# Gate and val products of the second MLP by Strassen's seven block products over pairs of token blocks

## The chip, the cores and the metric

The kernel runs on one core of one Trainium2 chip. The metric is the device time of one execution in microseconds (us). The kernel before was timed three times: 1830.27, 1833.56 and 1836.62 us, median 1833.56 us. A separate execution was profiled.

## The reference

Attention over pooled keys feeds two MLPs, and only the last result is returned:

```python
x = attention(q, pool8(k), pool8(v))          # 4608 tokens x 512
h = x @ w_in                                  # 512 x 2048
x = where(h >= 1, h, where(h <= -1, 0, (h + 1)**2 / 4)) @ w_out
gate = 1 / (1 + exp(-(x @ w_gate)))           # 512 x 1536
val = x @ w_val                               # 512 x 1536
out = (gate * val) @ w_out2                   # 1536 x 512
```

Every product is made to nearly full float32 accuracy: each operand is split into a high and a low part, and three matmuls (high x high, high x low, low x high) stand for one.

## The kernel before

The 4608 tokens are NB = 9 blocks of 512 columns, the model width 512 is KD = 4 chunks of 128 rows, the second MLP's width is M2 = 12 chunks. `three` (line 564) issues the three matmuls of one 128 x 128 weight block with one 128 x 512 operand; `columns` (line 569) does so for the four chunks of the width and leaves 12 matmuls in one PSUM bank. There are eight banks: four `acc`, two `h`, two `a`.

The first MLP leaves its transposed result of block j in DRAM as `y_d[j]`. The weights of the second MLP are decoded while the first MLP runs and go to DRAM as 36 `spilled` tensors of 256 KB. `reload` (line 503) brings one back, ScalarE (ACT) copies out the high part, VectorE (DVE) subtracts to get the low part. All 36 are reloaded once: eight into pool `w2a`, which opens when attention's pools are closed (`open_a`), sixteen into the slots of the first MLP's `win`, twelve into `w2b`, which opens when the first MLP's pools `wout` and `wj` are closed (`open_b`). From then on the weights stay in SBUF.

The loop from line 692 on goes over nine blocks and twelve m. For one m it issues 12 matmuls for gate into an `h` bank, 12 for val into an `a` bank, then sigmoid on ACT (line 700), the product with val on DVE (line 702), high part on ACT (line 491) and low part on DVE (line 500) into `g`, and two steps later 12 matmuls of `g` with `w2[2, m]` into the four `acc` banks. `x2_load` (line 674) fetches the next block's `y_d` in two DMAs. `out_rows` copies `acc` out and stores it.

The order of the instructions is not that of the code. Every operation goes to a `Plan` with an engine, a cost and a due time (`key`); `Plan.issue` lists them: on each engine, of those that could start first, the one with the smallest key goes next. The engines then run that order as it stands. SP issues the loads and stores, POOL the loads and spills of the second MLP's weights; each waits in order too.

Of the kernel before, what the change touches and what calls it, by code (L numbers as in the profile page):

```python
# [64 lines left out]
class Plan:  # L65
# [130 lines left out]
def pooled_attention_two_mlps(  # L196
# [53 lines left out]
    def buf_x(dtype=F32R, shape=(P, 2, TB)):  # L250
        return Buf(x_p, "x", 2 * KD, list(shape), dtype)
# [252 lines left out]
    def reload(d, t, key, behind):  # L504

        vals = Src(t, lambda t: t[:, 1].bitcast(F32))
        op(SP, 0.475, key - AHEAD_RELOAD, lambda: nc.sync.dma_start(out=vals(), in_=d.t),
           r=[d], w=[t], behind=behind, nbytes=P * DM * 4)
        op(ACT, 0.62, key - 2, lambda: nc.scalar.copy(out=t.t[:, 0], in_=vals()), r=[t], w=[t])
        op(DVE, 0.69, key - 1, lambda: nc.vector.tensor_tensor(  # L510
            out=t.t[:, 1], in0=vals(), in1=t.t[:, 0].bitcast(F32), op=ALU.subtract), r=[t], w=[t])
# [49 lines left out]
        return t.t.rearrange("p s (c f) -> p s c f", c=KD)  # L561


    def three(o, wh, wl, xh, xl, start, stop):
        nc.tensor.matmul(out=o, lhsT=wh, rhs=xh, start=start, stop=False)  # L565
        nc.tensor.matmul(out=o, lhsT=wh, rhs=xl, start=False, stop=False)  # L566
        nc.tensor.matmul(out=o, lhsT=wl, rhs=xh, start=False, stop=stop)  # L567

    def columns(key, o, w, xs):
        last = []  # L570
# [103 lines left out]
    def x2_load(j, key):
        raw = [buf_x(F32) for _ in range(2)]
        for i, r in enumerate(raw):
            op(SP, 0.475, key, lambda i=i, r=r: nc.sync.dma_start(
                out=r.t, in_=y_d[j].t[2 * i * P:2 * (i + 1) * P, :].rearrange("(c p) t -> p c t", p=P)),
                r=[y_d[j]], w=[r], nbytes=P * DM * 8)
        return raw  # L680

    def x2_split(raw, key):
        xs = []
        for c in range(KD):
            x, src = buf_x(), Src(raw[c // 2], lambda t, c=c: t[:, c % 2])
            high_part(key, x, src)
            low_part(key, x, src)
            xs.append(x)
        return xs

    xs = x2_split(x2_load(0, due1((NB - 1) * M1)), due1(NB * M1 - 2))
    for j in range(NB):
        raw = x2_load(j + 1, due2(j, 0)) if j + 1 < NB else None
        for m in range(M2):
            T = due2(j, m)
            pg, pv = bank("h", True), bank("a", True)
            columns(T, pg, w2[0, m], xs)
            columns(T + 2.6, pv, w2[1, m], xs)
            t, g = Buf(t_p, "t", 2, [P, TB]), buf_g()
            op(ACT, 0.48, T + 5, lambda t=t, pg=pg: nc.scalar.activation(out=t.t, in_=pg.t, func=AF.Sigmoid),  # L700
               r=[pg], w=[t])
            op(DVE, 0.6, T + 6, lambda t=t, pv=pv: nc.vector.tensor_tensor(  # L702
                out=t.t, in0=pv.t, in1=t.t, op=ALU.mult), r=[t, pv], w=[t])
            high_part(T + 7, g, Src(t))
            low_part(T + 8, g, Src(t))
            if m == 0:
                accs = [bank("acc") for _ in range(4)]
                last_o = [[] for _ in range(4)]
            w = w2[2, m]
            for c in range(4):  # L710
                def mm(c=c, w=w, g=g, m=m, accs=accs):
                    three(accs[c].t, g.t[:, 0, c * P:(c + 1) * P], g.t[:, 1, c * P:(c + 1) * P],
                          w.t[:, 0], w.t[:, 1], m == 0, m == M2 - 1)
                last_o[c] = [op(PE, 0.65, T + 2 * S2 + 5.2 + 0.1 * c, mm, r=[w, g], w=[accs[c]], behind=last_o[c])]
        if raw:
            xs = x2_split(raw, due2(j + 1, 0) - 1)
        out_rows(T + 2 * S2 + 6, out[j * TB:(j + 1) * TB, :], accs)
# [33 lines left out]
```

## Time and profile before

| what | value |
|---|---|
| times of three executions | 1830.27, 1833.56, 1836.62 us |
| profiled execution | 1831.4 us, of which 1829.6 us lie between first and last instruction (the span) |
| TensorE (PE) busy | 1787.8 us, 8096 matmuls of all sizes |
| weight loads (PEld) busy | 1447.3 us |
| DVE, ACT, POOL busy | 856.5, 763.1, 46.2 us |
| DMA | 122.01 MB, mean 67 GB/s |
| mean granted clock of TensorE | 0.993 of full speed |

Busy time is the sum over an engine's instructions where they don't overlap. Matmuls are pipelined: each lasts longer than the distance to the next. The granted clock is 1.00 at 2.4 GHz and 0.50 at 1.2 GHz; a mean between them is a mixture of the two.

### The profile page before, as it was taken

Reading aid. Unit: us, or ns where it says so; the run is one execution under the profiler, and the core shown is the slowest. Engines: PE = TensorE matmul, PEld = TensorE weight load, DVE = VectorE, ACT = ScalarE, POOL = GpSimd, SP = SyncE. Lnnn points to the kernel's source line nnn. Section 1 sums busy time; section 2 is a strip of 40 time slices with the busy share of each in tenths; the row PEclk is TensorE's granted clock in tenths of the full one; section 3 lists DMA queues with packets and bytes.
Section 4 is the critical chain, followed back from the end, with each engine's and each line's share of the span. In section 5 each row is a group of like instructions: output and inputs, shape, how many; then the busy total and the mean of one; then the engine's idle time right before and its main releaser. Section 6 shows DMA issues by size and latency. Waiting matters only on the chain.

```text
span 1829.6 us, 21475 instructions
## 1 busy us (share of the span) xinstructions
PE 1787.8 (98%) x8096; PEld 1447.3 (79%) x8096; DVE 856.5 (47%) x1581; ACT 763.1 (42%) x1719; POOL 46.2 (3%) x78
## 2 busy tenths in 40 slices
PE   6789999999999999999999999999999999999998
PEld 4567778888888777878888888888888888888887
DVE  8899767676776866566451212121121212121211
ACT  6766656565666656566561211121121212121111
POOL 0000001010100100010000000000000000000000
PEclk9999999999999999999999999999999999999999
DMA  8632525242433432123140000000010101010000
GB/s 215 203 102 75 144 56 163 60 143 73 133 89 113 115 90 70 59 77 116 47 144 1 23 24 23 24 23 24 1 46 1 46 1 47 0 47 0 1 23 24
DMA packets 136712, 122.01 MB, mean 67 GB/s; under 512 B 82592, under 2 KB 100000, under 8 KB 136608
## 3 DMA queue, kind: packets, MB, share of 16 engines
q1 hardware_dynamic: 128544, 92.32, 17.8%
q0 software_dynamic: 8064, 28.32, 4.6%
q8 instruction: 64, 1.05, 0.2%
q14 instruction: 40, 0.33, 0.1%
HBM read 82.84 MB, written 28.31 MB: 61 GB/s over the span
## 4 chain that ended last, share of the span: by engine, by line
PE 92%; DVE 2%; DMA 2%; ACT 2%; issue 1%; SPq 0%; POOL 0%; DVEq 0%; POOLq 0%; ACTq 0%
PE h L565 12%; PE acc L565 12%; PE acc L567 12%; PE acc L566 12%; PE h L567 12%; PE h L566 12%; PE a L565 5%; PE a L567 5%; PE a L566 5%; PE a L402 2%; PE a L470 2%; DMA win<-in_moe_w_in_dram 1%; DMA raw<-in_moe_w_out_dram 1%; ACT f L537 0%; DMA x<-in_k_dram 0%
## 5 line engine op out<-in xcount | busy, mean ns | idle before, releaser
L702 DVE TENSOR_TENSOR t<-a,t 128x512 f32<-128x512 f32 x108 | 74.7, 692 | 566.0 <-PE a L567 566.0
L567 PE MATMUL h<-x,win 128*128 128x512 f32 x756 | 297.2, 393 | 8.8 <-DVE win L500 8.8
L565 PE MATMUL h<-x,win 128*128 128x512 f32 x756 | 300.5, 398 | 0.0
L566 PE MATMUL h<-x,win 128*128 128x512 f32 x756 | 296.7, 393 | 0.0
L491 ACT CAST g<-t 128x512 fp32r<-128x512 f32 x252 | 156.6, 621 | 331.9 <-DVE t L702 274.1
L565 PE MATMUL acc<-g,wj 128*128 128x512 f32 x576 | 229.5, 399 | 2.1 <-ACT g L491 2.1
L567 PE MATMUL acc<-g,wj 128*128 128x512 f32 x576 | 225.9, 392 | 4.0 <-DVE wj L500 4.0
L700 ACT ACTIVATE t<-h 128x512 f32<-128x512 f32 x108 | 64.8, 600 | 386.7 <-PE h L567 386.7
L566 PE MATMUL acc<-g,wj 128*128 128x512 f32 x576 | 225.3, 391 | 0.2 <-DVE g L500 0.2
L500 DVE TENSOR_TENSOR g<-t,g 128x512 fp32r<-128x512 f32 x252 | 173.6, 689 | 107.5 <-ACT g L491 106.8
L630 ACT ACTIVATE t<-h,half 128x512 f32<-128x512 f32 x144 | 99.3, 689 | 185.7 <-PE h L567 185.7
L567 PEld LDWEIGHTS h<-x,win 128*128 128x128 f32 x756 | 143.2, 189 | 41.6 <-DVE win L500 11.6
L565 PEld LDWEIGHTS h<-x,win 128*128 128x128 f32 x756 | 144.0, 190 | 38.7 <-issue 5.9
L566 PEld LDWEIGHTS h<-x,win 128*128 128x128 f32 x756 | 143.4, 190 | 28.8
L634 DVE SCALAR_TENSOR_TENSOR t<-t,h 128x512 f32<-128x512 f32 x144 | 97.7, 679 | 89.6 <-ACT t L632 89.0
L567 PEld LDWEIGHTS acc<-g,wj 128*128 128x128 f32 x576 | 108.7, 189 | 28.9 <-DVE wj L500 6.1
L565 PEld LDWEIGHTS acc<-g,wj 128*128 128x128 f32 x576 | 109.0, 189 | 25.6 <-ACT g L491 2.5
L566 PEld LDWEIGHTS acc<-g,wj 128*128 128x128 f32 x576 | 108.8, 189 | 22.0 <-DVE g L500 0.5
L500 DVE TENSOR_TENSOR wj<-wout_f,wj 128x512 fp32r<-128x512 f32 x144 | 98.8, 687 | 24.5 <-ACT wj L491 24.5
L491 ACT CAST wj<-wout_f 128x512 fp32r<-128x512 f32 x144 | 89.7, 623 | 32.7 <-PE acc L567 31.8
L632 ACT ACTIVATE t<-t 128x512 f32<-128x512 f32 x144 | 91.2, 633 | 3.4
L565 PE MATMUL acc<-win,g 128*128 128x512 f32 x216 | 84.0, 389 | 0.0
(134 smaller groups left out, 2921.8 us busy)
## 6 DMA issues: line engine op xcount, KB each, us to landing
y<-raw SPq DMA_DIRECT2D x18, 512.0 KB
w<-f POOLq DMA_DIRECT2D x36, 256.0 KB, 2.3
x<-y SPq DMA_DIRECT2D x18, 512.0 KB
out_dram<-raw SPq DMA_DIRECT2D x18, 512.0 KB
win<-in_moe_w_in_dram SPq DMA_DIRECT2D x16, 512.0 KB
raw<-in_moe_w_out_dram SPq DMA_DIRECT2D x16, 512.0 KB
aT<-aq SPq DMA_DIRECT2D x256, 32.0 KB
kv<-in_k_dram SPq DMA_DIRECT2D x28, 288.0 KB
```

Of the source, the lines that this page charges most:

```text
L402: nc.tensor.matmul(out=view()[lo - r0:hi - r0, t].rearrange("p h c -> p (h c)"), lhsT=qT.t[:, lo:hi], rhs=bds[b % 2, p].t, start=True, sto ...
L470: nc.tensor.matmul(out=px.t[D * h:D * h + D, lo:hi], lhsT=vps[b % 2, p].t[:, h], rhs=rhs, start=True, stop=True)
L491: ACT: (0.52, lambda: nc.scalar.copy(out=dst.t[:, 0], in_=src())),
L500: op(engs, [0.6 if e == DVE else 1.23 for e in engs], key, [lambda e=e: by[e].tensor_tensor(out=dst.t[:, 1], in0=src(), in1=dst.t[:, 0].bi ...
L565: nc.tensor.matmul(out=o, lhsT=wh, rhs=xh, start=start, stop=False)
L566: nc.tensor.matmul(out=o, lhsT=wh, rhs=xl, start=False, stop=False)
L567: nc.tensor.matmul(out=o, lhsT=wl, rhs=xh, start=False, stop=stop)
L630: op(ACT, 0.69, Tg, lambda t=t, hps=hps: nc.scalar.activation(out=t.t, in_=hps.t, func=AF.Relu, bias=half.t, scale=0.5), r=[hps, half], w=[t])
L632: op(ACT, 0.63, Tg + 1, lambda t=t: nc.scalar.activation(out=t.t, in_=t.t, func=AF.Square), r=[t], w=[t])
L634: op(DVE, 0.69, Tg + 2, lambda t=t, hps=hps: nc.vector.scalar_tensor_tensor(out=t.t, in0=t.t, scalar=1.0, in1=hps.t, op0=ALU.min, op1=ALU. ...
L700: op(ACT, 0.48, T + 5, lambda t=t, pg=pg: nc.scalar.activation(out=t.t, in_=pg.t, func=AF.Sigmoid), r=[pg], w=[t])
L702: op(DVE, 0.6, T + 6, lambda t=t, pv=pv: nc.vector.tensor_tensor(out=t.t, in0=pv.t, in1=t.t, op=ALU.mult), r=[t, pv], w=[t])
```

## The change

Block 0 is computed as before. The other eight blocks are taken in four pairs (j1, j2). For a pair, a matrix n (0 gate, 1 val) and two neighbouring m (index i of 0 to 5), the product of a 2 x 2 arrangement of weight blocks (halves of the width by two m) with a 2 x 2 arrangement of token blocks is made from seven block products instead of eight, in Winograd's form of Strassen's algorithm. A block product is six matmuls (two chunks, three each). The seven go to four banks A, B, C, D: products 4, 5 and 6 are added in PSUM onto the results of products 0, 2 and 3, which ACT or DVE have read in between. One (pair, n, i) is called a step below: 42 matmuls where there were 48, and 48 steps in all.

The seven weight matrices of a step (three of the four blocks as they are, four sums) with high and low parts make a tile of 128 x 3584 floats, 1.835 MB. `prepare` makes it while block 0 is computed: two loads from `spilled` into the slot and one of the fourth block into `f`; four adds on DVE (line 737); the splits (lines 686, 687, 691, 692); a store to DRAM (`seven`) on POOL's queue. Block 0 uses the same slot's first three matrices and `f`. The pairs read the tiles back by `load_seven` (SP, line 753), 12 for a pair. All this goes through three slots in turn, two `wa` (in place of `w2a`) and one `wb` (in place of `w2b`). The twelve `w_out2` tiles stay in SBUF as before.

The seven operands on the token side of a pair are made by `minus` (line 832) and the splits; they lie in `x`, two `win` slots each for T1 and T4, and `xb` for the last. After the products DVE and ACT make the four results: `add` (line 877), sigmoid (line 889), the product (line 896). These wait in `gs` (12 tiles), and `out_part` (line 765) splits them and multiplies with `w_out2`, over half a pair later.

```diff
-    def three(o, wh, wl, xh, xl, start, stop):
+    def three(o, wh, wl, xh, xl, start, stop, more=False):
...
+    PSTEP = 11 * 2.6
+    PAIR0 = due2(1, 0) + 1
+    NPR, MP = (NB - 1) // 2, M2 // 2
...
+    NMAT, HK = 7, 2 * P
+    seven = [fixed(dram.tile([P, 2 * NMAT * HK], F32, name=f"seven{n}")) for n in range(2 * MP)]
+    def buf_seven():
+        tag, bufs = (("wa", 2), ("wa", 2), ("wb", 1))[turn[0] % 3]
+        turn[0] += 1
+        return late(tag, bufs, [P, 2, NMAT, HK], F32R)
+    def prepare(n, i, key):
...
+        comb(0, A21, lambda: lo(2), ALU.add)
+        comb(1, lambda: sm.t[:, 0], lambda: lo(0), ALU.subtract)
+        comb(2, lambda: lo(0), A21, ALU.subtract)
+        comb(3, lambda: lo(1), lambda: sm.t[:, 1], ALU.subtract)
+        split2(key - 3, lambda: a21.t[:, 0], lambda: a21.t[:, 1], 0.38, a21)
+        split2(key - 3, lambda: sl.t[:, 0, 0:3], lambda: sl.t[:, 1, 0:3], 1.0, sl)
+        split_to(key - 1, lambda: sm.t, lambda: sl.t[:, 0, 3:], lambda: sl.t[:, 1, 3:], 1.3, sm, sl)
+        d = seven[2 * i + n]
+        op2(PL, 1.0, key + 1, lambda: nc.gpsimd.dma_start(out=d.t, in_=...), r=[sl], w=[d], nbytes=...)
...
+            for n in range(2):
+                T = T0p + PSTEP * i + PSTEP / 2 * n
+                H = PSTEP / 14
+                sl = load_seven(n, i, T - 24)
...
+                A, Bk, Ck, Dk = bank("h", True), bank("a", True), bank("h", True), bank("a", True)
+                s1 = Buf(f_p, "f", 3, [P, TB])
+                u2, u3 = (late("u", 3, [P, TB]) for _ in range(2))
+                product(0, A, 0, B11, True)
+                op(ACT, 0.6, T + H * 1, lambda s1=s1, A=A: nc.scalar.copy(out=s1.t, in_=A.t), r=[A], w=[s1])
+                product(1, Bk, 4, T2, True)
+                add(T + H * 2, u2, Bk, s1)
+                product(2, Ck, 5, T3, True)
+                add(T + H * 3, u3, Ck, u2)
+                product(3, Dk, 3, T1, True)
+                finish(T + H * 4, (1, 1), Dk, u3)
+                product(4, A, 1, B21, False)
+                finish(T + H * 5, (0, 0), A, None)
+                product(5, Ck, 2, T4, False)
+                finish(T + H * 6, (1, 0), Ck, u2)
+                product(6, Dk, 6, B22, False)
+                finish(T + H * 7, (0, 1), Dk, u2)
...
+        for b in range(2):
+            accs = [bank("acc") for _ in range(4)]
+            for m in range(M2):
+                out_part(gss[b, m], m, T0p + PSTEP * (3.4 + (M2 * b + m) / 4), accs, lasts, 40)
```

TensorE's list has 7568 rows of this kind before and 7280 with the change; up to the end of attention the orders are alike. Three places follow.

DVE at the end of the first MLP, before (the row of `wj` is the last weight split of the first MLP, the rows of `raw` copy its last result out, those of `w2b` are low parts of reloaded weights, `t` and `g` belong to block 0 of the second MLP):

```order
L500 TENSOR_TENSOR wj<-wout_f_130,wj 128x512
L500 TENSOR_TENSOR x<-x 128x512
L510 TENSOR_TENSOR win<-win 128x512
...
L583 COPY raw<-acc 128x512 x2
L510 TENSOR_TENSOR w2b<-w2b 128x512 x7
L702 TENSOR_TENSOR t<-a,t 128x512
```

The same place with the change (`raw` now also holds the four weight sums, `xb`, `u`, `x` and `win` with one operand `u` belong to the first pair's token side):

```order
L500 TENSOR_TENSOR wj<-wout_f_130,wj 128x512
L737 TENSOR_TENSOR raw<-f,wb 128x256
L737 TENSOR_TENSOR raw<-raw,wb 128x256
L832 TENSOR_TENSOR u<-xb,x 128x512
L737 TENSOR_TENSOR raw<-wb,f 128x256
L832 TENSOR_TENSOR u<-xb,u 128x512
L737 TENSOR_TENSOR raw<-wb,raw 128x256
L832 TENSOR_TENSOR u<-win,u 128x512
L687 TENSOR_TENSOR x<-x 128x512
L687 TENSOR_TENSOR f<-f 128x256
L687 TENSOR_TENSOR wb<-wb 128x768
```

The `wb` rows, on which block 0's fifth group of 12 matmuls depends, stand between rows of the first pair's operands; the first `t<-a,t` of before (now `gs<-a,t`) comes eight rows further down, and the first low part of `g` seven rows behind that.

DVE inside a pair, one step of gate and one of val (`u` are partial sums, `t` and `f` what the sigmoid gets, `gs` the results):

```order
L877 TENSOR_TENSOR u<-a,f 128x512
L877 TENSOR_TENSOR u<-h,u 128x512
L877 TENSOR_TENSOR t<-a,u 128x512
L877 TENSOR_TENSOR f<-h,u 128x512
L877 TENSOR_TENSOR f<-a,u 128x512
...
L877 TENSOR_TENSOR gs<-a,u 128x512
L896 TENSOR_TENSOR gs<-gs,t 128x512
L896 TENSOR_TENSOR gs<-h,t 128x512
L877 TENSOR_TENSOR gs<-h,u 128x512
L896 TENSOR_TENSOR gs<-gs,f 128x512
```

Five rows for gate and nine for val (two `u` rows ahead of the `gs` rows, a last add and product behind them) stand where before there were one `t<-a,t` and one `g<-t,g` for each m.

SP in block 0 with the change (a slot's loads: four blocks of weights in three DMAs; where before two `x<-y` loads and two stores a block were the whole list):

```order
L723 DMA wb<-w_6_153 128x512
L725 DMA wb<-w_9_156 128x256
L758 DMA xb<-y_108 128x512 x4
...
L727 DMA f<-w_10_157 128x256
L723 DMA wa<-w_7_154 128x512
L725 DMA wa<-w_10_157 128x256
```

Between the two parts stand the two stores of the first MLP's last block, so the next slot's loads wait behind stores that wait for copies on ACT and DVE.

## Rows read from the trace of the kernel before

**Rows 1.** The page, part 1: busy us, share of the span, instructions.
```profile
PE 1787.8 (98%) x8096; PEld 1447.3 (79%) x8096; DVE 856.5 (47%) x1581; ACT 763.1 (42%) x1719; POOL 46.2 (3%) x78
```

**Rows 2.** The page, part 4: the chain that ended last, shares by engine.
```profile
PE 92%; DVE 2%; DMA 2%; ACT 2%; issue 1%; SPq 0%; POOL 0%; DVEq 0%; POOLq 0%; ACTq 0%
```

**Rows 3.** The view of windows: us, busy time of each engine, clock, DMA share, GB/s.
```profile
100.00:200.00 100.00, 89.84 (x391) 68.89 (x391) 90.37 (x188) 65.91 (x161) 1.66 (x2) 0.93 0.38 106
200.00:930.00 730.00, 729.28 (x3458) 587.09 (x3457) 489.75 (x924) 443.81 (x1063) 43.85 (x70) 1.00 0.33 93
930.00:1080.00 150.00, 150.00 (x664) 124.11 (x663) 43.35 (x65) 42.33 (x71) 0.00 (x0) 1.00 0.16 53
1080.00:1260.00 180.00, 180.00 (x796) 149.10 (x795) 37.01 (x54) 35.40 (x59) 0.00 (x0) 1.00 0.07 24
```

**Rows 4.** The timeline of SP, 1000 to 1300 us: start, us, operation.
```profile
1032.12 1.11 SPq L677 DMA_DIRECT2D x<-y  x2
...
1130.04 1.07 SPq L677 DMA_DIRECT2D x<-y  x2
...
1227.96 1.07 SPq L677 DMA_DIRECT2D x<-y  x2
```

**Rows 5.** Groups of DVE by shape: busy us, mean ns, idle before.
```profile
L500 DVE TENSOR_TENSOR g<-t,g 128x512 fp32r<-128x512 f32 x252 | 173.6, 689 | 107.5 <-ACT g L491 106.8
...
L702 DVE TENSOR_TENSOR t<-a,t 128x512 f32<-128x512 f32 x108 | 74.7, 692 | 566.0 <-PE a L567 566.0
...
L320 DVE TENSOR_TENSOR kv<-kv 72x256 f32<-72x256 f32 x56 | 23.3, 416 | 0.6
```

**Rows 6.** Groups of ACT by shape.
```profile
L491 ACT CAST g<-t 128x512 fp32r<-128x512 f32 x252 | 156.6, 621 | 331.9 <-DVE t L702 274.1 <-DVE t L634 57.5
...
L700 ACT ACTIVATE t<-h 128x512 f32<-128x512 f32 x108 | 64.8, 600 | 386.7 <-PE h L567 386.7
```

**Rows 7.** The timeline of DVE, 926 to 930 us.
```profile
927.40 0.69 DVE L500 TENSOR_TENSOR g<-t,g 128x512 fp32r<-128x512 f32 x1 [0.69 <-ACT g L491]
928.02 0.69 DVE L500 TENSOR_TENSOR wj<-wout_f,wj 128x512 fp32r<-128x512 f32 x1
928.62 0.69 DVE L510 TENSOR_TENSOR win<-win 128x512 fp32r<-128x512 f32 x1
```

**Rows 8.** The timeline where the first MLP ends, 943 to 947 us.
```profile
943.25 0.39 PE L567 MATMUL acc<-g,wj 128*128 128x512 f32 x1
...
943.67 3.71 SPq L507 DMA_DIRECT2D w2b<-w  x6
...
946.57 0.63 ACT L509 CAST w2b<-w2b 128x512 fp32r<-128x512 f32 x1 [3.66 <-DMA w2b<-w]
```

**Rows 9.** The view of windows in loads of `y` alone (1132 to 1134).
```profile
1132.00:1133.00 1.00, 1.00 (x6) 0.83 (x5) 0.31 (x2) 0.63 (x1) 0.00 (x0) 1.00 0.86 326
1133.00:1134.00 1.00, 1.00 (x6) 0.82 (x5) 0.48 (x1) 0.27 (x1) 0.00 (x0) 1.00 0.91 309
```

**Rows 10.** The view of windows in stores alone (1151 to 1153).
```profile
1151.00:1152.00 1.00, 1.00 (x6) 0.84 (x5) 0.00 (x0) 0.04 (x1) 0.00 (x0) 1.00 1.03 401
1152.00:1153.00 1.00, 1.00 (x6) 0.81 (x6) 0.00 (x0) 0.00 (x0) 0.00 (x0) 1.00 1.07 416
```

**Rows 11.** The view of windows, weight loads and stores mixed (952 to 954).
```profile
952.00:954.00 2.00, 2.00 (x11) 1.65 (x10) 1.03 (x2) 1.97 (x3) 0.00 (x0) 1.00 0.85 234
```

**Rows 12.** DMA issues of POOL: KB each, us from issue to landing.
```profile
w<-f POOLq DMA_DIRECT2D x36, 256.0 KB, 2.3
```

More of the change, by code (lines that the diff above doesn't have):

```diff
@@ L561, in view_cols @@
         return t.t.rearrange("p s (c f) -> p s c f", c=KD)
[L564 to L567 removed]
+    def three(o, wh, wl, xh, xl, start, stop, more=False):
+        nc.tensor.matmul(out=o, lhsT=wh, rhs=xh, start=start, stop=False, skip_group_check=more)
+        nc.tensor.matmul(out=o, lhsT=wh, rhs=xl, start=False, stop=False, skip_group_check=more)
+        nc.tensor.matmul(out=o, lhsT=wl, rhs=xh, start=False, stop=stop, skip_group_check=more)
     def columns(key, o, w, xs):
@@ L674, in x2_load @@
[L674 to L717, printed above, removed]
@@ new lines, in late, with op2, buf_win @@
+    def late(tag, bufs, shape, dtype=F32, fifo=True):
+        b = Buf(lambda: pools2["wa" if tag == "wa" else "right"], tag, bufs, shape, dtype, fifo)
+        b.behind = [open_a if tag == "wa" else open_b]
+        return b
+    def op2(eng, cost, key, fn, r=(), w=(), behind=(), **kw):
+        more = [x for b in w if not b.users for x in b.behind]
+        return op(eng, cost, key, fn, r=r, w=w, behind=list(behind) + more, **kw)
+    def buf_win(behind):
+        b = Buf(win_p, "win", M1, [P, 2, TB], F32R)
+        b.behind = behind
+        return b
@@ new lines, in split2, with split_to @@
+    def split2(key, out_hi, out_lo, cost, b):
+        op2(ACT, cost, key, lambda: nc.scalar.copy(out=out_hi(), in_=out_lo().bitcast(F32)), r=[b], w=[b])
+        op2(DVE, cost, key + 0.5, lambda: nc.vector.tensor_tensor(
+            out=out_lo(), in0=out_lo().bitcast(F32), in1=out_hi().bitcast(F32), op=ALU.subtract), r=[b], w=[b])
+    def split_to(key, val, out_hi, out_lo, cost, src, b):
+        op2(ACT, cost, key, lambda: nc.scalar.copy(out=out_hi(), in_=val()), r=[src, b], w=[b])
+        op2(DVE, cost, key + 0.5, lambda: nc.vector.tensor_tensor(
+            out=out_lo(), in0=val(), in1=out_hi().bitcast(F32), op=ALU.subtract), r=[src, b], w=[b])
@@ new lines, in load_seven, with x_raw, x_split @@
+    def load_seven(n, i, key):
+        sl, d = buf_seven(), seven[2 * i + n]
+        op2(SP, 0.475, key, lambda: nc.sync.dma_start(
+            out=sl.t.rearrange("p s k f -> p (s k f)").bitcast(F32), in_=d.t), r=[d], w=[sl], nbytes=P * 2 * NMAT * HK * 4)
+        return sl
+    def x_raw(x, part, j, c, key):
+        op2(SP, 0.475, key, lambda: nc.sync.dma_start(
+            out=x.t[:, part].bitcast(F32), in_=y_d[j].t[c * P:(c + 1) * P, :]), r=[y_d[j]], w=[x], nbytes=P * TB * 4)
+    def x_split(x, key):
+        split2(key, lambda: x.t[:, 0], lambda: x.t[:, 1], 0.69, x)
@@ new lines, in out_part, with mm @@
+    def out_part(gs, m, key, accs, last, ahead=5):
+        g = buf_g()
+        op2(ACT, 0.62, key - ahead, lambda: nc.scalar.copy(out=g.t[:, 0], in_=gs.t), r=[gs], w=[g])
+        op2(DVE, 0.69, key - ahead + 1, lambda: nc.vector.tensor_tensor(
+            out=g.t[:, 1], in0=gs.t, in1=g.t[:, 0].bitcast(F32), op=ALU.subtract), r=[gs, g], w=[g])
+        w = w2[m]
+        for c in range(4):
+            def mm(c=c):
+                three(accs[c].t, g.t[:, 0, c * P:(c + 1) * P], g.t[:, 1, c * P:(c + 1) * P],
+                      w.t[:, 0], w.t[:, 1], m == 0, m == M2 - 1)
+            last[c] = [op(PE, 0.65, key + 0.1 * c, mm, r=[w, g], w=[accs[c]], behind=last[c])]
@@ new lines, in buf_gs, with mm @@
+    def buf_gs():
+        return late("gs", 12, [P, TB], fifo=False)
+    lasts = [[] for _ in range(4)]
+    xs = [buf_x() for _ in range(KD)]
+    for c in range(KD):
+        x_raw(xs[c], 1, 0, c, due1((NB - 1) * M1))
+    for c in range(KD):
+        x_split(xs[c], due1(NB * M1 - 2))
+    accs = [bank("acc") for _ in range(4)]
+    for i in range(MP):
+        slots = [prepare(n, i, due2(0, 2 * i) - 6 + 2.6 * n) for n in range(2)]
+        T = due2(0, 2 * i)
+        banks = {(n, f): bank("ha"[n], True) for n in range(2) for f in range(2)}
+        for n in range(2):
+            sl, a21 = slots[n]
+            for f in range(2):
+                last = []
+                for c in range(KD):
+                    def mm(c=c, sl=sl, a21=a21, o=banks[n, f], f=f):
+                        k = slice(c % 2 * P, c % 2 * P + P)
+                        a = [a21.t[:, s, k] if (f, c // 2) == (1, 0) else
+                             sl.t[:, s, {(0, 0): 0, (0, 1): 1, (1, 1): 2}[f, c // 2], k] for s in range(2)]
+                        three(o.t, a[0], a[1], xs[c].t[:, 0], xs[c].t[:, 1], c == 0, c == KD - 1)
+                    last = [op(PE, 0.65, T + 5.2 * n + 2.6 * f + 0.1 * c, mm, r=[sl, a21, xs[c]], w=[banks[n, f]], behind=last)]
+        for f in range(2):
+            m = 2 * i + f
+            t, gs = Buf(t_p, "t", 2, [P, TB]), buf_gs()
+            op(ACT, 0.6, T + 2.6 * f + 5, lambda t=t, pg=banks[0, f]: nc.scalar.activation(out=t.t, in_=pg.t, func=AF.Sigmoid),
+               r=[banks[0, f]], w=[t])
+            op2(DVE, 0.69, T + 2.6 * f + 6, lambda t=t, gs=gs, pv=banks[1, f]: nc.vector.tensor_tensor(
+                out=gs.t, in0=pv.t, in1=t.t, op=ALU.mult), r=[t, banks[1, f]], w=[gs])
+            out_part(gs, m, due2(0, m) + 2 * S2 + 5.2, accs, lasts)
```

116 lines of the change are left out of this document (105 added, 11 removed).

## The prediction, made before the changed kernel ran

> **What bounds the kernel.** I read the busy times first: PE is busy in 98% of the span, DVE in 47%, ACT in 42% [rows 1]. A busy PE could still wait inside, so next the chain that ended last: 92% of it is PE, 2% DMA [rows 2]. Then the stages. From 930 us on, which is where the second MLP runs, PE is busy in all of 150 and of 180 us, at a granted clock of 1.00 (2.4 GHz), while DVE works 37 of 180 us and the DMA engines move 24 GB/s [rows 3]. So in this stage nothing but matmuls sets the time, and what the change takes from them is gained unless it makes PE wait. The beat is in SP's timeline: the load of the next block comes every 97.92 us (1130.04 less 1032.12, and 1227.96 less 1130.04) [rows 4]. A block has 12 x 36 = 432 matmuls, so one takes 97.92 / 432 = 0.2267 us. Nine blocks are 881.3 us.
>
> The sum is made against the profiled execution, 1831.4 us. It lies 2.2 us below the median of the three timed runs and inside their 1830.27 to 1836.62; I add nothing for that.
>
> **What is removed.** 4 pairs x 12 steps x 6 = 288 matmuls. The operand is 128 x 512 in all of them and the weights are again 128 x 128, so the distance stays 0.2267 us: 65.3 us less. The second MLP would take 97.9 + 4 x 792 x 0.2267 = 816 us. This is the most that can come: PE has no idle time there to win back.
>
> The Trainium skill ("TensorE: Matmul & The Clock Gate", section "Wait — 56ns, not 53.3ns?") puts back-to-back matmuls of N columns at N / 2.4 GHz + 2.5 ns, 215.8 ns for 512. By that figure, as an estimate, the 288 would be worth 62.1 us. The trace differs: 226.7 ns here, and I use that.
>
> **What is added beside PE, and what hides it.**
> (a) *Pairs, vector work.* Two steps (gate and val) have 84 matmuls of products and bring 48 of `out_part`, 29.9 us. DVE does 14 rows for them and 4 low parts, 18 x 0.69 = 12.4 us [rows 5]; ACT 2 copies, 4 sigmoids, 4 high parts, 10 x 0.61 = 6.1 us [rows 6]. Where steps follow without out parts it is 9.7 us of 19.0. Both are covered by PE.
> The waits inside a step: a product is 6 x 0.2267 = 1.36 us. Product 5 writes bank C again and needs `u3`, which has read C. Product 0 ends at 1.5, ACT's copy at 2.2, `u2` after product 1 at 3.6, `u3` after product 2 at 5.0; product 5 starts at 6.8. Product 6 needs bank D read after product 3: done at 6.3, start at 8.2. So 1.8 us are to spare, between two and three DVE instructions. I cost it at nothing.
> (b) *Pairs, loads.* 48 tiles of 1.835 MB. A first 256 KB is there 2.9 us after its release (matmul 943.25 + 0.39, first use 946.57) [rows 8]; the rest at 326 GB/s [rows 9] takes 4.8 us, 7.7 together. Three slots leave at least two steps, 19.0 us, between release and next use. Cost nothing; without that cover each load would cost up to 7.7 us.
> (c) *Pair boundaries, three of them.* `xb` comes free only when the last product of a pair is done, and everything derived from it is late. The order puts 72 matmuls of out parts there, 16.3 us. The second product of the new pair comes 87 matmuls after the release, 19.7 us; its last operand is some 20 DVE rows behind the landing, 3.5 + 20 x 0.69 = 17.3 us. Covered, with little left for the third: I take 0.5 us each, 1.5 us, between 0 and 5.
> (d) *End of the first MLP.* The slot `wb` opens with the last matmul that reads `wj`. Two slots made earlier give PE 48 matmuls, 10.9 us. Meanwhile: second DMA landed 3.5 us after release, then DVE up to the row `wb<-wb` 4 x 0.42 + 4 x 0.69 + 0.42 + 1.04 (768 wide, from 0.69 for 512) = 5.9, at 9.4 us. Covered. Not so the first low part of `g`: 15 rows on, 8 of 6.2 us and 7 of 4.0, at 19.6 us, or 17.5 at the closest distance that DVE shows, 0.60 us [rows 7]. PE wants it after 74 matmuls, at 16.8. I take a wait of 1.5 us, between 0.7 and 2.8. Before it, two slots of 4.5 us of DVE work squeeze into the last steps of the first MLP: 1 us, between 0 and 2.
> (e) *Block 0.* DVE: 10 slots x 4.5 + 24 x 0.69 + 22 x 0.69 for the first pair's operands = 77 us of 97.9; tight, but not over. A slot's round: loads 4.1, preparation about 8 among the other rows, store 2.3 for the first 256 KB [rows 12] and 3.9 for the rest at 408 GB/s [rows 10], 18.3 us; three slots at 8.16 us a slot allow 24.5. The DMA engines move 10 x (0.52 + 1.835) + 2.1 + 1.0 = 26.7 MB, 273 GB/s. Loads alone ran at 309 to 326, stores alone at 401 to 416, both mixed at 234 [rows 9 to 11]. By the first two it is 70 us, hidden; by the last 114 us, 16 more than PE needs. The mixed row is the nearest in kind, but its stretch had few bytes waiting at a time (share 0.85), so I take it as hidden and keep 16 us as the other end.
> POOL's queue holds nothing but the twelve stores by then; SP's loads wait behind two stores of the first MLP, which I have in (d).
>
> **Sum.** 1831.4 - 65.3 + 1.5 (c) + 1.5 + 1.0 (d) = **1770 us**. Own bounds: with no wait at all 1766, less 3 for the spread of the runs, 1763; with the upper ends of (c) and (d) and 3 us in block 0, 1779.
>
> **Rivals.**
> 1. *Block 0 becomes the bound.* Stores and loads share the engines at 234 GB/s, slots come late, and PE waits about once for each slot: + 16 us, 1786, with the small waits 1779 to 1795. For it: 273 GB/s is more than the mixed row, and DVE is at 79%. Against: stores alone ran at over 400, and a slot's round has 6 us to spare.
> 2. *The step's chain does not fit.* Each of 48 steps waits for DVE. A chain late by 1.8 us costs nothing, beyond that each us costs 48 us: at 1.8 + 1.3 = 3.1 us (between four and five DVE rows more than counted) the gain of 61 us is gone. The stretch from 100 to 200 us shows how it looks when DVE cannot follow: DVE busy 90, PE 90 of 100 us and the granted clock at 0.93, partly 1.2 GHz [rows 3]. If the four pairs went so, idle time (10%) and clock (7%) would add 17% of 718 us: 1770 + 122 = **1892 us**, slower. Against: DVE would need about 90% there and has 12.4 of 29.9 us.
> The Trainium skill has a rule that speaks for it (same page, section "A second HAM failure mode: psum-queue depth-cycling"): a kernel that cycles through PSUM banks idles PE between groups so often that its clock swings between the two levels. From 200 us on, with `h` and `a` used in turn, this trace does not show it: 1.00 throughout; no run here has banks added onto after being read.
> 3. *Part of this*: 0.2 to 1.2 us lost in each step, 1795 to 1826.
> That the matmuls are not really fewer is excluded by the order, 7280 rows for 7568.
>
> **Chances.** The forecast 0.62; rival 1 0.22; rival 3 0.08; within 0.3% of 1831 (5.5 us, about what a measurement of this kernel tells from no change) 0.03; slower, by rival 2, 0.05. Forecast and rival 1 make 0.84, so the range is 1763 to 1795. Faster by over 0.3%: 0.62 + 0.22 + 0.08 = 0.92.
>
> **What would show it.** Right: PE busy in all of every window from the second pair on, clock 1.00, a pair every 792 x 0.2267 = 179.5 us; on PE's list of waits, a few us in all for `g` and for `wb`. DVE near 50% there, near 80% in block 0, DMA near 270 GB/s in block 0 and 120 in the pairs. Rival 1: PE waits for DVE `wa` or `wb` or for their DMAs in block 0 alone. Rivals 2 and 3: PE waits on `h` and `a` for DVE `u` in the pairs. What would prove me wrong altogether is a distance of matmuls other than 0.227 us while nothing is waited for.

## The result and the profile after

The changed kernel takes 1774.16 us (median of 4 runs, 1773.89 to 1777.72); the kernel before 1834.26 us (median of 4). The ratio is 0.9679, 95% interval 0.9658 to 0.9700: 60 us less. The forecast of 1770 us lies 4 us low, the range of 1763 to 1795 holds the time.

The profiled execution took 1777.72 us, 1776.0 of them span. Its page, part 1 (busy us, share of the span, instructions) and part 4 (chain), against [rows 1, 2]:

```profile
PE 1726.7 (97%) x7808; PEld 1395.6 (79%) x7808; DVE 1077.2 (61%) x1933; ACT 816.7 (46%) x1807; POOL 52.5 (3%) x90
...
PE 91%; DVE 3%; DMA 2%; ACT 2%; issue 1%; SPq 1%; POOL 0%; DVEq 0%; ACTq 0%; POOLq 0%
```

There are 288 matmuls fewer and PE is busy 61.1 us less; DVE works 221 us more, and its share of the chain goes from 2% to 3%. The kernel is still bound by TensorE.

The view of windows (us, busy time of PE, PEld, DVE, ACT, POOL, granted clock, DMA share, GB/s) takes block 0 of the second MLP first, then the four pairs; it answers to [rows 3]:

```profile
950.00:1035.00 85.00, 81.81 (x354) 67.19 (x354) 61.00 (x108) 37.63 (x60) 4.79 (x9) 0.98 0.75 278
1035.00:1215.00 180.00, 180.00 (x796) 149.10 (x795) 86.28 (x129) 50.86 (x86) 0.53 (x1) 1.00 0.53 194
1215.00:1395.00 180.00, 180.00 (x796) 149.10 (x795) 87.43 (x132) 48.00 (x82) 0.00 (x0) 1.00 0.41 149
1395.00:1575.00 180.00, 180.00 (x796) 149.10 (x795) 87.56 (x133) 47.98 (x81) 0.00 (x0) 1.00 0.41 149
1575.00:1755.00 180.00, 180.00 (x796) 149.10 (x795) 78.33 (x116) 40.40 (x66) 0.00 (x0) 1.00 0.28 104
```

In all four pairs PE is busy without a gap at clock 1.00, DVE at 44 to 49%, the DMA engines at 104 to 194 GB/s. Only the first stretch lacks something: 3.19 of its 85 us, and a part of the clock.

How long a pair is stands in SP's timeline, where the loads of `xb` mark the third and the fourth pair:

```profile
1373.57 1.74 SPq L758 DMA_DIRECT2D xb<-y  x4
...
1553.09 1.74 SPq L758 DMA_DIRECT2D xb<-y  x4
```

That is 179.52 us for 792 matmuls, 0.2267 each, against 97.92 us for the 432 of a block before [rows 4].

The list of PE's waits from 930 us on has one row, and the timeline of PE shows it where it stands (start, us, operation, idle time before it and what ended it):

```profile
PE acc L568 <- DVE g L768: 3.2, 1, 3.2
```

```profile
949.82 0.39 PE L568 MATMUL acc<-g,wj 128*128 128x512 f32 x1
...
966.60 0.40 PE L567 MATMUL acc<-win,g 128*128 128x512 f32 x1
970.20 0.50 PE L568 MATMUL acc<-win,g 128*128 128x512 f32 x1 [3.19 <-DVE g L768]
970.53 0.39 PE L566 MATMUL acc<-win,g 128*128 128x512 f32 x1
```

The first row is the last matmul of the first MLP; it ends at 950.21. From its end to the end of the span is what I call the second MLP below: 1776.0 - 950.2 = 825.8 us here, and 1829.6 - 943.6 = 886.0 before [rows 8]. The wait is that for the first low part of `g`, term (d). Behind it a window shows a clock between the two levels of 1.2 and 2.4 GHz:

```profile
970.00:975.00 5.00, 4.80 (x14) 3.81 (x15) 5.00 (x11) 4.29 (x8) 0.00 (x0) 0.66 0.42 158
```

5 x (1 - 0.66) = 1.7 us are lost there. So the second MLP is 886.0 - 65.3 + 3.2 + 1.7 = 825.6 by terms and 825.8 by the trace. A stop also costs a little more than its row says: from 966.60 to 970.20 lie 3.60 us, 3.37 more than the usual 0.23 between two starts, and the next start follows after 0.33, together 0.28 us more than the 3.19 listed. The traces leave no room for another cost of the change in this stage.

Why the low part is late shows on DVE and SP. DVE's timeline:

```profile
954.95 0.43 DVE L737 TENSOR_TENSOR raw<-f,wb 128x256 f32<-128x256 f32 x1 [8.79 <-DMA wb<-w]
...
960.63 0.69 DVE L584 COPY raw<-acc 128x512 f32<-128x512 f32 x1
...
967.24 0.43 DVE L737 TENSOR_TENSOR raw<-f,wa 128x256 f32<-128x256 f32 x1 [1.19 <-DMA wa<-w]
...
969.45 0.69 DVE L768 TENSOR_TENSOR g<-gs,g 128x512 fp32r<-128x512 f32 x1
```

and SP's:

```profile
950.24 0.32 SPq L723 DMA_DIRECT2D wb<-w  x1
...
951.09 2.87 SPq L758 DMA_DIRECT2D xb<-y  x4
954.05 7.70 SPq L585 DMA_DIRECT2D y<-raw  x2
961.84 0.42 SPq L727 DMA_DIRECT2D f<-w  x1
```

The weights of `wb` reach DVE 4.7 us after the release. The two stores of the first MLP's last block hold SP's queue for 7.70 us, because the second one waits for the copy into `raw` that DVE makes at 960.63. Only then are the next slot's loads issued, and DVE, which works in order, waits 1.19 us for them at 967.24 while the low part of `g` stands five rows further down. It is done at 970.14, 19.9 us after the first MLP's end; PE had reached it at 967.0, 16.8 us after it.

### The profile page after: what moved, and what is told of

It is laid out like the page before. It is cut to its first block, busy times and chain, and to the rows that moved or that the text cites. A ratio compares the mean times of both kernels' runs of the same rounds, so it can differ in the third digit from the quotient of the medians.

```text
span 1776.0 us, 21678 instructions
## 1 busy us (share of the span) xinstructions
PE 1726.7 (97%) x7808; PEld 1395.6 (79%) x7808; DVE 1077.2 (61%) x1933; ACT 816.7 (46%) x1807; POOL 52.5 (3%) x90
## 4 chain that ended last, share of the span: by engine, by line
PE 91%; DVE 3%; DMA 2%; ACT 2%; issue 1%; SPq 1%; POOL 0%; DVEq 0%; ACTq 0%; POOLq 0%
PE acc L566 13%; PE acc L568 13%; PE acc L567 12%; PE h L566 12%; PE h L568 12%; PE h L567 12%; PE a L566 4%; PE a L567 4%; PE a L568 4%; PE a L402 2%; PE a L470 2%; DMA raw<-in_moe_w_out_dram 1%; DMA q<-in_q_dram 0%; DMA x<-in_k_dram 0%; DVE f L547 0%
## 5 line engine op out<-in xcount | busy, mean ns | idle before, releaser
L568 PE MATMUL h<-x,win 128*128 128x512 f32 x576 | 228.3, 396 | 8.8 <-DVE win L500 8.8
L566 PE MATMUL h<-x,win 128*128 128x512 f32 x576 | 231.6, 402 | 0.5 <-ACT win L491 0.3
L567 PE MATMUL h<-x,win 128*128 128x512 f32 x576 | 227.6, 395 | 0.0
L767 ACT CAST g<-gs 128x512 fp32r<-128x512 f32 x108 | 66.8, 622 | 318.1 <-PE acc L568 201.2
L568 PE MATMUL acc<-win,g 128*128 128x512 f32 x432 | 168.8, 391 | 3.2 <-DVE g L768 3.2
L566 PE MATMUL acc<-win,g 128*128 128x512 f32 x432 | 168.8, 391 | 0.0
L567 PE MATMUL acc<-win,g 128*128 128x512 f32 x432 | 168.6, 390 | 0.0
L768 DVE TENSOR_TENSOR g<-gs,g 128x512 fp32r<-128x512 f32 x108 | 74.2, 690 | 135.2 <-ACT g L767 135.0
L568 PEld LDWEIGHTS h<-x,win 128*128 128x128 f32 x576 | 110.0, 191 | 34.9 <-DVE win L500 11.5
L566 PEld LDWEIGHTS h<-x,win 128*128 128x128 f32 x576 | 110.8, 192 | 32.9 <-issue 5.9
L567 PEld LDWEIGHTS h<-x,win 128*128 128x128 f32 x576 | 110.0, 191 | 21.9
L500 DVE TENSOR_TENSOR g<-t,g 128x512 fp32r<-128x512 f32 x144 | 98.8, 686 | 37.0 <-ACT g L491 36.4
L491 ACT CAST g<-t 128x512 fp32r<-128x512 f32 x144 | 89.1, 619 | 56.7 <-DVE t L635 56.3
```

What stands on the lines that cost most here:

```text
L500: op(engs, [0.6 if e == DVE else 1.23 for e in engs], key, [lambda e=e: by[e].tensor_tensor(out=dst.t[:, 1], in0=src(), in1=dst.t[:, 0].bi ...
L767: op2(ACT, 0.62, key - ahead, lambda: nc.scalar.copy(out=g.t[:, 0], in_=gs.t), r=[gs], w=[g])
L768: op2(DVE, 0.69, key - ahead + 1, lambda: nc.vector.tensor_tensor(out=g.t[:, 1], in0=gs.t, in1=g.t[:, 0].bitcast(F32), op=ALU.subtract), r ...
```

## The experiments

All times are medians; each kernel was compared with the kernel before on the same chip. "Waits" are PE's from 930 us on. The shifts of line numbers between kernels come from the edits.

### Twice product 6: is the gain the number of matmuls?

```diff
                 product(6, Dk, 6, B22, False)
+                product(6, Dk, 6, B22, False)
```

> Edit: the seventh block product of each step is issued twice, so a step has 48 matmuls again; the added product is summed twice, so the output differs in that part. Everything else of the change stays (loads, stores, adds). Theory A (the gain is the count of matmuls at 0.2267 us and nothing else): 288 matmuls more, +65.3 us, 1774.2 to about 1839.5, that is 5 us over the kernel before, and no wait of PE in the pairs. Theory B (the rest of the change costs PE something that the shorter steps hide, or the adds and loads profit from longer steps): clearly more or less than 65 us, outside 60 to 70.

Measured: 1837.54 us, ratio 1.0022 (1.0011 to 1.0033). PE's waits and a pair's window:

```profile
PE acc L568 <- DVE g L768: 2.7, 1, 2.7
```

```profile
1035.00:1215.00 180.00, 180.00 (x796) 149.04 (x795) 78.31 (x116) 40.57 (x68) 0.00 (x0) 1.00 0.45 166
```

Everything that the change adds on DVE, ACT and the queues is there, only the 288 matmuls are back (product 6 now counts twice in the output), and with them the gain is gone: 63.4 us. The second MLP is 890.5 us, 64.7 more than in the changed kernel at a wait that is 0.5 shorter: 65.2 us for 288 matmuls, 0.226 us each. Theory A holds. The gain is the matmuls, and the beside-work costs nothing as long as PE has 42 or 48 matmuls in a step.

### The adds made twice and four times: how much room has a step's chain?

```diff
+                def again(key, o, b, u):
+                    for _ in range(1):
+                        op2(DVE, 0.0, key, lambda: nc.vector.tensor_tensor(out=o.t, in0=b.t, in1=u.t, op=ALU.add),
+                            r=[b, u], w=[o])
...
                 add(T + H * 2, u2, Bk, s1)
+                again(T + H * 2, u2, Bk, s1)
...
                 add(T + H * 3, u3, Ck, u2)
+                again(T + H * 3, u3, Ck, u2)
```

With `range(1)` two DVE rows are added to the chain that product 5 waits for, with `range(3)` six.

> Edit: the two adds of a step that lie between its products (u2, u3) are each made twice, the planner counts the repeats as free. The chain to product 5 grows by 1.2 to 1.4 us. Theory A (1.8 us to spare in the tightest steps, more where out parts stand in between): no wait, time within 2 us of 1774.2. Theory B (the chain is already at its edge, the waits just do not show in the list): each us costs up to 48 us, so +20 to +60 us.

> Edit: the same two adds are made four times each. The chain grows by about 4 us: u3 is ready about 1 us after product 5 could start in the 16 steps that have 12 matmuls between products 2 and 5; the other 32 steps have out parts there too, 24 matmuls, and keep about 1.7 us to spare. Theory A (only the 16 tight steps wait): +10 to +25 us, waits of PE on h for DVE, in the tight steps alone. Theory B (every step waits, as rival 2 of the prediction priced it): 48 x 1 us and more, +50 to +100 us. In both, an idle PE may bring the clock down, which would show as a granted clock below 1.00 in the pairs.

Measured with two rows more: 1773.74 us, ratio 0.9672 (0.9655 to 0.9689), the changed kernel's time. Of PE's idle rows in the pairs the first stands for three, one at each boundary (the others at 1392.49 and 1572.66):

```profile
1212.33 0.50 PE L566 MATMUL h<-win,wa 128*128 128x512 f32 x1 [0.35 <-DVE u L882]
```

The second MLP is 826.1 us, 0.3 more than in the changed kernel: 1.1 us of such waits come in, and the 1.7 us of half clock behind the wait for `g` are missing here (last section). Theory A holds for the time; three steps do wait. Why these three shows in the changed kernel's own rows, `u3` on DVE and the first matmul of product 5 on PE, for a step of the first pair with no `out_part` in its chain and for the first step of the second pair:

```profile
1066.90 0.69 DVE L877 TENSOR_TENSOR u<-h,u 128x512 f32<-128x512 f32 x1 [0.60 <-PE h L568]
1069.42 0.39 PE L566 MATMUL h<-win,wa 128*128 128x512 f32 x1
...
1219.22 0.69 DVE L877 TENSOR_TENSOR u<-h,u 128x512 f32<-128x512 f32 x1 [0.38 <-PE h L568]
1220.38 0.39 PE L566 MATMUL h<-win,wa 128*128 128x512 f32 x1
```

In the former `u3` is done at 1067.59 and PE comes at 1069.42: 1.83 us to spare, and 1.8 was the prediction's figure. Twelve of the 48 steps are like this, with two products (12 matmuls) between product 2 and product 5. In the first step of the second, third and fourth pair the order takes product 3 ahead of product 2, only six matmuls lie between, and the room is 1220.38 - 1219.91 = 0.47 us. In the very first step it is 3.2 us, in the other 32, where 12 matmuls of `out_part` come in besides, 4.55 us.

With six rows more: 1830.65 us, ratio 0.9983 (0.9969 to 0.9996). The whole gain is gone. PE's waits, then windows of two pairs:

```profile
PE h L566 <- DVE u L882: 33.4, 16, 3.3
PE acc L568 <- DVE g L768: 2.7, 1, 2.7
```

```profile
1035.00:1215.00 180.00, 167.91 (x697) 135.75 (x696) 118.15 (x174) 33.82 (x58) 0.53 (x1) 0.95 0.44 163
1215.00:1395.00 180.00, 172.91 (x746) 141.68 (x746) 125.81 (x190) 46.63 (x80) 0.00 (x0) 0.98 0.37 135
```

Two rows are 1.2 to 1.4 us and fit into the 1.8 us of (a); six are 3.6 to 4.1 and don't. But not 48 steps wait, only 16. The twelve with 1.83 us of room wait 1.92 us each, which is what six rows are over it; the first steps of the last three pairs, with 0.47, wait 3.25; the very first step of all waits 0.56; the 32 steps with `out_part` in between don't wait. And the price isn't the waits alone. The granted clock is below 1.00 in every pair: 180 us x (0.05 + 0.02 + 0.03 + 0.02) is 22 us by the windows of the four. Waits of 33.4 and about 22 us of clock are 55 of the 56.5 us by which the second MLP is longer than in the changed kernel. So theory A is right on which steps wait, but its 10 to 25 us are too small: the waits are 1.9 us where it had 1, and the clock comes on top. Theory B's 50 to 100 us hold the time, but not for its reason.

### Twice the load: how much cover have the seven tiles?

```diff
-        op2(SP, 0.475, key, lambda: nc.sync.dma_start(
-            out=sl.t.rearrange("p s k f -> p (s k f)").bitcast(F32), in_=d.t), ...)
+        for _ in range(2):
+            op2(SP, 0.475, key, lambda: nc.sync.dma_start(
+                out=sl.t.rearrange("p s k f -> p (s k f)").bitcast(F32), in_=d.t), ...)
```

> Each of the 48 loads of a seven tile in the pairs is issued twice into the same slot, the second one waiting for the first (86 MB more through the queue; the result is the same). Theory A, the prediction's (b): a load takes 7.7 us and is issued some 19 us before its first product, one tile per 15 us (180 us of a pair over 12 tiles), so two loads one behind the other (14 to 16 us) still land in time: 1774, within 3 us, PE without a wait on wa or wb in the pairs, DMA at 300 GB/s and more there. Theory B: the loads already land near their time of use (other traffic stretches them), so the second one is late by several us in most tiles: 48 x 2 to 4 us, 1870 to 1970, with PE waits on DMA wa and wb in the chain.

Measured: 1789.16 us, ratio 0.9752 (0.9736 to 0.9768), the second MLP 15 us longer. Windows of the first two pairs, PE's waits for the tiles, and the waits of SP's queue from 1035 us on:

```profile
1035.00:1215.00 180.00, 171.59 (x741) 139.17 (x740) 75.83 (x114) 42.81 (x72) 0.53 (x1) 0.99 0.82 319
1215.00:1395.00 180.00, 179.52 (x791) 148.04 (x790) 87.25 (x132) 47.90 (x81) 0.00 (x0) 1.00 0.74 272
```

```profile
PE h L566 <- DMA wb<-seven: 3.4, 3, 1.9
PE h L566 <- DMA wa<-seven: 2.8, 3, 1.3
```

```profile
SPq L754 <- DMA wa<-seven: 273.8, 31, 13.2
SPq L754 <- PE a L568: 177.0, 31, 16.0
SPq L754 <- DMA wb<-seven: 143.3, 16, 11.9
```

The page has 88.1 MB more than that of the changed kernel (322.3 against 234.2). Neither theory holds in whole. In the last three pairs A does: PE idles 0.5, 0.7 and 0 us of 180 there, with twice the bytes. In the first pair B does: PE idles 8.4 us, where the DMA engines move 319 GB/s, the last store of block 0 and the loads of the next pair's operands among it. A first load of the two held SP's queue (273.8 + 143.3) / 47 = 8.9 us on average, up to 13.2, where I had 7.7. A tile comes due every 15 us (180 / 12), and beside these waits the queue still stood 177.0 us for PE to free a slot: over the four pairs the loads are ahead of PE even so. Of the 15 us, some 9 are waits that the changed kernel doesn't have (12.6 in all less its 3.0 on `g`) and 1.8 are clock in the first pair (0.91 in 20 us). The other 4 us are mostly what stops cost beyond their rows: 0.28 us each, as at the first wait for `g` above, is 3.6 us for the 13 waits of the pairs.

### Twice the store: how much room have the DMA engines in block 0?

```diff
+    spare = [fixed(dram.tile([P, 2 * NMAT * HK], F32, name=f"spare{n}")) for n in range(2 * MP)]
...
+        d2 = spare[2 * i + n]
+        op2(PL, 1.0, key + 1, lambda: nc.gpsimd.dma_start(out=d2.t, in_=sl.t...), r=[sl], w=[d2], ...)
```

> Each of block 0's 12 seven tiles is stored twice, the second time to a DRAM tensor that nothing reads (22.0 MB more in block 0; the result is the same). In the changed kernel 950 to 1035 us shows 278 GB/s at a DMA share of 0.75, so full engines would move about 371 GB/s there, and 23.6 MB + 22.0 MB need 110 (at the 416 GB/s of the store rows) to 123 us, against 85. Theory A, that block 0's transfers are hidden but with little room: the DMA becomes the bound and the kernel takes 1799 to 1812, waits of DVE on slots of wa and wb whose stores are late, PE waiting behind them. Theory B, that the room is large (transfers overlap with others better than the share says): below 1780. Theory C, that the transfers of block 0 were already part of the bound of the changed kernel: the whole second store adds itself, 22.0 MB / 0.37 to 0.42 = 53 to 59 us, 1827 or more.

Measured: 1795.26 us, ratio 0.9783 (0.9762 to 0.9804), the second MLP 847 us, 21 more. A window in block 0 and two of PE's idle rows:

```profile
1020.00:1040.00 20.00, 17.82 (x78) 14.08 (x76) 9.22 (x16) 4.74 (x8) 2.11 (x4) 1.00 1.01 413
```

```profile
1011.99 0.79 PE L566 MATMUL a<-x,wa 128*128 128x512 f32 x1 [7.55 <-ACT wa L686]
...
1063.03 0.80 PE L566 MATMUL h<-x,wa 128*128 128x512 f32 x1 [5.26 <-DMA wa<-seven]
```

The mechanism is A's: the engines are full (share about 1.0 at 400 to 413 GB/s), slots come late (SP's loads into them wait 51.8 us in all for second stores to land), PE waits behind them, 7.55 us once in block 0 and 5.26 at the first pair's first load. It is rival 1, made to happen. Loads and stores together, most of them stores, ran at the rate of stores alone [rows 10] and not at 371 GB/s. The time is 4 us below A's lower end, which already took 416 GB/s; why isn't shown. Nor does the run tell full engines from a slot's longer round, since each slot also comes free only after its second store.

### The first pair's token side held back, and the copy of the last block moved

Three kernels look for the 5 us at the first MLP's end. First the DVE and ACT work of the first pair's operands is held until block 0's second low part of `g`:

```diff
+        if eng in (ACT, DVE):
+            more += hold
...
-        op2(DVE, 0.69, key - ahead + 1, lambda: nc.vector.tensor_tensor(
+        lows.append(op2(DVE, 0.69, key - ahead + 1, lambda: nc.vector.tensor_tensor(
...
+        hold[:] = [lows[1]] if pr == 0 else []
```

> Edit: DVE's and ACT's work on the first pair's token operands is held back until block 0's second low part of g is listed. Theory A (what is missing from 65.3 us is one wait of PE for the low part of g, 3.2 us, and the 3.4 us at half clock that follow it, 1.7 us): both go, PE's list of waits is empty from 930 us on, the clock stays at 1.00, and the time falls by 4.9 us, from 1774.2 to about 1769. Theory B (the wait only moves: the operands or the next slot are late instead): another wait of 2 to 5 us shows up in block 0 or at the start of the first pair, and the time stays within 2 us of 1774.

Measured: 1774.71 us, ratio 0.9677 (0.9662 to 0.9691): no gain, and the second MLP is 826.3 us. Theory B holds: the wait moves. PE's waits, then the rows of DVE and ACT that stand ahead of them:

```profile
PE h L566 <- ACT t L813: 1.7, 1, 1.7
PE acc L568 <- DVE g L774: 1.5, 2, 1.2
PE a L568 <- DVE wa L691: 1.4, 1, 1.4
```

```profile
956.86 0.69 DVE L584 COPY raw<-acc 128x512 f32<-128x512 f32 x1 [3.25 <-DMA y<-raw]
...
957.46 1.22 DVE L696 TENSOR_TENSOR wb<-raw,wb 128x1024 fp32r<-128x1024 f32 x1
```

```profile
956.91 0.59 ACT L583 COPY raw<-acc 128x512 f32<-128x512 f32 x1 [3.42 <-DMA y<-raw]
957.51 1.28 ACT L813 ACT_TABLE_LOAD   x1
```

DVE is free earlier, but both engines then stand 3.3 us in front of the copy of the last block's second half: its tile `raw` is the one that the first `y` store still reads. The sigmoid, the weight split and the low part queue behind that copy. In the changed kernel neither engine stands idle in front of this copy (DVE makes it at 960.63 above): the token side's rows ahead of it fill the time.

So the copy was given two tiles of its own (in `gs`, which block 0 doesn't need yet), and the token side was spread, four operations behind each low part of `g`:

```diff
+            if i and d and d[0] is y_d[NB - 1]:
+                for n, a in enumerate(accs[2:]):
+                    st = late("gs", 12, [P, TB], fifo=False)
...
+                continue
             st = Buf(raw_p, "raw", 2, [P, 2, TB])
...
-        if eng in (ACT, DVE):
-            more += hold
+        if hold and eng in (ACT, DVE):
+            more.append(lows[min(2 + hold[0] // 4, 10)])
+            hold[0] += 1
```

> From the run with the held token side: the token side of the first pair is spread over block 0 (four operations behind each low part of g), and the second half of the first MLP's last block goes from PSUM into two tiles of its own instead of the raw tile that waits for the first store, so that ACT's sigmoid and DVE's first product no longer stand behind that copy. Theory A (the whole loss at the first MLP's end is that copy and the token side ahead of g): the waits of 1.2 to 1.7 us go, second MLP 821 to 822.5 us, 1769.5 to 1771.5. Theory B (what is late next is the landing of the weights of block 0's first pair of tiles, 4.7 us behind the store rows on the same queue, and then wa's own loads): a wait of 1 to 3 us stays on another tile of block 0, 1772.5 to 1776.

Measured: 1768.15 us, ratio 0.9639 (0.9619 to 0.9660). The list of PE's waits after 930 us is empty, and the window with block 0 shows no gap:

```profile
930.00:1035.00 105.00, 105.00 (x465) 86.97 (x464) 67.84 (x117) 48.14 (x76) 5.33 (x10) 1.00 0.69 255
```

ACT's timeline shows the copy at once behind the last result and the sigmoid's table 7.7 us after the first MLP's end, where it was 10.6 us with the token side held alone:

```profile
946.82 0.59 ACT L584 COPY gs<-acc 128x512 f32<-128x512 f32 x1 [0.47 <-PE acc L568]
...
954.50 1.28 ACT L826 ACT_TABLE_LOAD   x1
```

The first MLP ends at 946.8, the second takes 1767.8 - 946.8 = 821.0 us, 4.8 less than in the changed kernel and what 886.0 - 65.3 = 820.7 allows. Theory A holds for the stage; the time lies 1.4 us under its 1769.5.

Then the spread was taken away again, and the staged kernel and the changed kernel were run beside it:

```diff
-        hold[:] = [0] if pr == 0 else []
```

> From the staged kernel, the spread of the first pair's token side is taken away again; the two staging tiles stay. Theory A (copy and token side are two causes, each enough to make the first low part of g late): DVE has about 11 us of combinations, splits and token-side work between the landing of wb (4.7 us after the last matmul of the first MLP) and its first product, so the low part of g is done at 18.5 to 19 us after that matmul, and PE wants it at 16.8: a wait of 1.7 to 2.2 us stays, second MLP 822.7 to 825 us, 1770 to 1773. Theory B (the copy that waits for the store was the whole cause in the changed kernel too): no wait, second MLP 821 us, the same time as the staged kernel within 1 us.

> The changed kernel once more, on one chip with the two kernels beside it. Both theories: 1774 within 3 us, a wait of about 3 us on the first low part of g, second MLP 825 to 826 us.

> The kernel with staging tiles and spread token side once more, beside the two others. Both theories: no wait of PE after the first MLP, second MLP 821 us, 4 to 6 us below the changed kernel.

Measured on one chip: staging alone 1773.55 us (ratio 0.9667, 0.9653 to 0.9680), the changed kernel 1774.54 (0.9677, 0.9660 to 0.9693), staging with the spread 1770.02 (0.9647, 0.9634 to 0.9660). PE's idle rows with staging alone, and a window behind them:

```profile
962.70 0.50 PE L566 MATMUL acc<-win,g 128*128 128x512 f32 x1 [0.52 <-ACT g L786]
...
964.86 0.50 PE L568 MATMUL acc<-win,g 128*128 128x512 f32 x1 [1.42 <-DVE g L787]
```

```profile
965.00:970.00 5.00, 5.00 (x15) 3.92 (x16) 5.00 (x9) 3.11 (x5) 0.00 (x0) 0.66 0.57 194
```

Waits of 1.9 us stay, as theory A has it (1.7 to 2.2), plus 1.7 us of clock that it didn't count: the second MLP takes 825.3 us, just over A's 822.7 to 825. So there are two causes, and taking away either alone gains nothing that can be measured; both together gain 4.5 us on this chip and 4.4 us of the second MLP (821.1 against 825.5). One step of this is not tested: without the staging tiles the token side was held back, never spread, and some of what PE then waits for (1.4 us on `wa`) may come from the work held back. The version with both is the best of this study, 3.5% below the kernel before.

## Why the prediction was right, point by point

**The removed matmuls, -65.3: right.** Distance 0.2267 us in the pairs (179.52 / 792), and 65.2 us when the 288 were put back. The Trainium skill's formula ("TensorE: Matmul & The Clock Gate", section "Wait — 56ns, not 53.3ns?") gives 215.8 ns, 62.1 us by the prediction's estimate. That is again not what these rows show.

**(a) The step's chain, 0: right.** No wait on `h` or `a` in the pairs. The room of 1.8 us is 1.83 by the trace in the twelve steps that the working fits. It took the products in the order of the code, though, and in the first step of three pairs PE's order leaves 0.47 us: there the zero was a near thing, and two rows more cost 0.35 us. DVE was forecast near 50% in the pairs and is at 44 to 49%.

**(b) Loads, 0: right**, though a load is longer than I had it (8.9 us where a second one follows it, not 7.7). It takes twice the load to lose time, and then mostly in the first pair.

**(c) Pair boundaries, +1.5: 0 measured.** I had 17.3 us of work against 19.7 us of cover and kept half a microsecond for each. No wait came. At the first boundary the second product starts at 1213.58 us and the last low part of its operand is done at 1211.76: 1.8 us to spare, where I had 2.4. So the allowance was not needed; the tight place at a boundary is the chain of (a).

**(d) End of the first MLP, +1.5 and +1.0: this is the term that was mis-sized.** The second part, slots that squeeze into the first MLP's last steps, cost nothing: PE is busy in all of 800 to 943 us before and after, at clock 1.00. The first cost 3.2 us and 1.7 us of clock, 4.9 together, where I had 1.5 and 2.8 as the upper end. I had the low part at 17.5 to 19.6 us after the first MLP's end; it came at 19.9. At the closest distance of DVE's rows, 17.5, two things were missing: `wb` landed at 4.7 and not 3.5 us (+1.2), and DVE waited 1.19 us for `wa`, whose loads stood behind the `y` stores on SP. Under (e) I had put those stores down to (d), but in (d) I only counted DVE's rows. And I had no price for the clock behind a wait. (c) and (d) together were forecast at 4.0 and came out at 4.9 us: 2.4 too little in (d), and 1.5 too much in (c), which happened to make up for part of it.

**(e) Block 0, 0: right.** From 950 to 1035 us the DMA share is 0.75 and PE waits for no slot; DVE, forecast near 80%, is busy 61.0 of 85 us. In the doubled-store run loads and stores together, most of them stores, moved 400 to 413 GB/s. So the 234 GB/s of [rows 11] was not the limit, though its share was 0.85; why so little moved there is open. By 400 GB/s the 26.7 MB of block 0 need 67 us, close to the 70 that I took.

**The rest.** 825.8 us for the second MLP against 886.0 - 65.3 + 4.0 = 824.7 forecast. The median came out 4.2 us above 1770, the second MLP 1.1. Most of the rest is where the sum starts: 1831.4 us is 2.9 below the median before, 1834.26, and I added nothing for that.

**The rivals.** Rival 1 didn't come, and needs 22 MB more in block 0 to come. Rival 2 was rightly unlikely, but its price was wrong: I let each microsecond beyond 1.8 cost 48 us. Of 48 steps only 16 wait when the chain grows by six rows, so a microsecond beyond costs some 16 us of waits; the clock then adds two thirds to that. Six rows more, 2 us over in most of these steps, did take the whole gain. The Trainium skill ("TensorE: Matmul & The Clock Gate", section "A second HAM failure mode: psum-queue depth-cycling") tells of a kernel that cycles through PSUM banks and idles TensorE between groups so often that its clock goes back and forth between its two levels. The run with six rows more agrees in part: PE idles between groups of one bank and the next, and the granted clock of whole pairs is 0.95 to 0.98. The changed kernel goes through the same four banks at 1.00, so the cycling by itself doesn't do it. Rival 3 didn't come either; its lower end was worked out wrongly, since 0.2 us in each of 48 steps gives 1780 and not 1795.

## What to carry to other kernels

In a stage where PE has no gap, matmuls removed were worth their distance, and work added beside them cost nothing until the one chain that the matmuls wait for ran out of room; count that room in instructions, in the order that the engines really get, at the steps with the least between. At a seam between two stages, don't only count the late engine's rows: look for a copy or a store in the same in-order queues that waits for an earlier DMA, since everything behind it waits too. When two such causes cover one another, removing either shows nothing; take away both before concluding that the place is worth nothing.

## What the runs showed that I had not expected

**The clock after a short wait.** The same wait for `g` at the first MLP's end was followed by a window of 5 us at 0.66 in the changed kernel (wait 3.19 us), and with staging alone (1.42 us behind one of 0.52). The windows of the runs with product 6 twice, the adds four times, the doubled load and the doubled store also lack about 1.7 us there. In the run with adds made twice it was not so, at a wait just as long:

```profile
963.93 0.50 PE L568 MATMUL acc<-win,g 128*128 128x512 f32 x1 [3.12 <-DVE g L768]
```

```profile
965.00:970.00 5.00, 5.00 (x24) 4.13 (x23) 4.97 (x9) 3.23 (x6) 0.07 (x1) 1.00 0.47 138
```

Nor was it after the 1.7 and 1.4 us of the run with the token side held. The wait's length alone doesn't tell whether the 1.7 us of half clock follow; what decides stays open.

**The first MLP ends at different times.** Its last matmul starts at 943.25 us before [rows 8] and at 949.82 in the changed kernel's profile; in the other runs it starts between 943.15 (twice product 6) and 948.34 us, and the changed kernel itself, profiled a second time, has it at 945.34. The difference doesn't come from the change: the 600th matmul recorded starts at 180.3 us before and at 187.0 after, and from there to the last of the first MLP it is 762.9 and 762.8 us. That is as large as all the small terms of the sum, and why times were compared by the length of the second MLP in the traces wherever a few microseconds mattered.
